# Gated unit, second half of the rows: both parts of a product (14 products of 512 columns), then four down accumulations together

## The chip, the cores and the metric

One Trainium2 chip, one of its cores. The time is device microseconds (us) of one execution of the program, from start to end. The kernel before takes 2795.59 us (median of 3 runs, 2795.36 to 2797.85).

## The reference, cut to what matters

An adaLN-conditioned block: layer norm, attention with 32 heads, residual, layer norm again, and a gated unit. The change lies in the gated unit, for 2048 rows `s`, width 576 and hidden width 4608:

```python
g = jnp.einsum("bsd,df->bsf", x, w_gate)
u = jnp.einsum("bsd,df->bsf", x, w_up)
h = _sigmoid(g) * u
return jnp.einsum("bsf,fd->bsd", h, w_down)
```

## The kernel before, in words

**Blocks and halves.** The hidden width is cut into `NB` = 18 blocks of 256, the rows into two halves of 1024. For each half and block the gate product and the up product are made as a Strassen-like scheme of seven products, in the order `ORDER = (1, 6, 2, 7, 5, 4, 3)`; the list `seq` holds all of them, and the loop `for n, (hf, b, k) in enumerate(seq)` runs one step for each.

**A product.** `product(st, k, acc, first, halves)` (L1221 to L1228) makes for each part `v` (0 is gate, 1 is up) seven matmuls of 512 columns into one PSUM bank `acc[v]`; all are line L1225. Its banks come from five that are used in turn (`product_bank`, tiles `x`). Weights of a step come by a DMA on SP's queue, asked for four steps ahead (L1197), into one of five buffers.

**The second half.** For blocks 1 to 16 (`SEVENS`) of the second half, the flag `sevens` is set and the loop goes through its own branch, 16 x 7 = 112 steps. There the down product of the block before is made by seven products too, one in each step: `sevenths(j, b, tiles)` (L1300 to L1319) makes, for each of four row tiles, one accumulation of three matmuls of 288 columns (L1307) into a bank of the pool `pd`, and adds it on VectorE to an SBUF sum (`G` at L1313, `Oa` at L1316 and L1319). `pd` has three buffers (tiles `d`), used in turn, so the accumulation of a row tile takes the bank of the one three before it, and its first weight load waits until VectorE has added that one.

```python
for t in tiles:
    acc = pd.tile([P, 512], F32, name="d")[:, 0:HALF]
    for n, (a, k) in enumerate(((h, 0), (h, 1), (l, 0))):
        nc.tensor.matmul(acc, a[:, rows], w[:, k, :], start=n == 0, stop=n == 2)
```

**What else VectorE and ScalarE do in a step of this branch.** An add of the bank of each part to an SBUF operand (L1660, in steps 6, 7, 5, 4, 3); in steps 2, 5, 4, 3 ScalarE's sigmoid of the gate part (`gate`, L1236, or L1234 for step 2) and at the step's end VectorE's product of the two parts (`gate_high`, L1242 or L1244), then ScalarE's rounded copy (L1249); `flush()` makes the rest to that copy on VectorE (`gate_low`, L1254). In step 1 `sums_of(before)` makes four sums of the block before on VectorE, in two pieces: s1 and s2 (L1335, L1336) ahead of the first product, S4 and s3 (L1340, L1341) at the second `next(made)`; S4 needs s2, s2 needs s1, s1 needs step 3's product of the two parts. `high` (L1322) copies each of them on ScalarE, `low` (L1327) makes its rest on VectorE in steps 6, 2 and 7. In step 1 ScalarE also copies the two banks to `p1` (L1668, L1676).

**The order.** From step 7 of `seq` on a manual schedule holds TensorE, VectorE and ScalarE to the order in which the program writes their instructions; nothing is moved by a planner. Each engine works its own queue in order and waits for the others by semaphores. SP's and POOL's queues carry the DMAs.

**Names used below.** p0 and p1 are the seven matmuls of part 0 and of part 1. t0 to t3 are the four row tiles of a step's down accumulations, and "the add of t0" is VectorE's add for it. add0 and add1 are VectorE's adds of the two parts at L1660.

Of the kernel before, what the change touches and what calls it, by code (L numbers as in the profile page):

```python
# [15 lines left out]
F32 = mybir.dt.float32  # L16
# [7 lines left out]
P = 128  # L24
# [37 lines left out]
TURNS = {1: 1, 6: 2, 2: 4, 7: 3, 5: 5, 4: 7, 3: 6}  # L62
# [25 lines left out]
def tile_block(ctx, tc, x_in, wqkv, wo, w_gate, w_up, w_down, c_in, w_mod, out):  # L88
    nc = tc.nc
# [911 lines left out]
    def load_block(pool, b, k, tied=None):  # L1001


        f0 = b * 256
        r0 = k * HALF
        raw = pool.tile([P, 2, 3, 256], F32, name=f"raw{k}", bufs=1 + k)
        queue = nc.gpsimd if tied else nc.sync
        for v, w in enumerate((w_gate, w_up)):
            loads = queue.dma_start(
                raw[:, v, 0:2, :], w[r0 : r0 + 256, f0 : f0 + 256].rearrange("(t p) c -> p t c", p=P)  # L1010
            ), queue.dma_start(
                raw[:, v, 2, :],
                w[r0 + 256 : r0 + HALF, f0 : f0 + 256].unsqueeze(0).to_broadcast([4, 32, 256]),
            )
            if tied:
                for load in loads:
                    tied(load)
        return raw
# [20 lines left out]
    for u in range(UNITS):  # L1039
        half, p = divmod(u, H // 2)  # L1040
# [5 lines left out]
        for kt in range(NT):  # L1046
# [43 lines left out]
            if u in (1, 3):  # L1090
                if kt == 0:
                    a = big.tile([P, 8, 640], F32, name="big")
                    a = a.rearrange("p a b -> p (a b)")[:, 0 : 8 * D].rearrange("p (t c) -> p t c", t=4)
                    b = slots.tile([P, 2560], F32, name="w0")[:, 0 : 2 * D]
# [21 lines left out]
            if u == 30 and kt == 7:  # L1116
                first = [load_block(raws, b, k, paced) for b, k in ((0, 0), (0, 1), (1, 1))]
# [31 lines left out]
    def region(name):  # L1149
        return ctx.enter_context(tc.tile_pool(name=name, bufs=1))  # L1150

    ep = region("ep")
# [68 lines left out]
    def product(st, k, acc, first, halves=(0, 1)):  # L1221
        s, w = ORDER.index(k), st["w", k]
        for v in halves:
            for n, (a, b) in enumerate(((0, 0), (0, 3), (3, 0), (1, 1), (1, 4), (4, 1), (2, 2))):
                nc.tensor.matmul(  # L1225
                    acc[v], w[:, v, a, :], X[s][:, b, :],
                    start=first and n == 0, stop=n == 6, skip_group_check=not first,
                )  # L1228

    def gate(st, t):  # L1230

        if t is None:
            t = ep2.tile([P, 512], F32, name="sg")
            nc.scalar.activation(t, st["a"][0], AF.Sigmoid)  # L1234
        else:
            nc.scalar.activation(t[:, 0:512], t[:, 0:512], AF.Sigmoid)  # L1236
        return t
# [14 lines left out]
    def gate_low(st, t, f, r):  # L1252

        nc.vector.tensor_sub(st["hl", r][:, f, :], t, st["hh", r][:, f, :].bitcast(F32))  # L1254
# [13 lines left out]
    def rows_of(j):  # L1268

        r, f = {1: (0, 0), 2: (0, 1), 4: (1, 1), 5: (1, 0)}.get(j, (None, None))  # L1270
        if r is None:
            i = {3: 0, 6: 1, 7: 2}[j]
            return late["hx"][:, i, :], late["lx"][:, i, :]
        return late["hh", r][:, f, :], late["hl", r][:, f, :]

    def columns_of(j):

        q = {1: (0, 0), 2: (1, 0), 3: (1, 1)}.get(j)
        if q:
            return late["wd"][:, :, q[0], q[1] * HALF : (q[1] + 1) * HALF]  # L1280
        i = {5: 0, 6: 1, 7: 2, 4: 3}[j]
        return late["wt"][:, i // 2, :, i % 2, :]
# [17 lines left out]
    def sevenths(j, b, tiles):  # L1300

        (h, l), w = rows_of(j), columns_of(j)
        for t in tiles:
            rows = slice(t * P, (t + 1) * P)
# [3 lines that stand above are left out]
            if j in late["G"]:  # L1308
                to = late["G"][j][:, t, :]
                if b == 0:  # L1310
                    nc.vector.tensor_copy(to, acc)
                else:
                    nc.vector.tensor_add(to, to, acc)  # L1313
            elif j == 4:
                to = Oa[:, 4 + t, 0:HALF]
                nc.vector.tensor_sub(to, to, acc)  # L1316
            else:
                to = Oa[:, t, 0:HALF] if j == 2 else Oa[:, t, HALF:D]
                nc.vector.tensor_add(to, to, acc)  # L1319
# [5 lines left out]
    def low(j):  # L1325
        h, l = rows_of(j)
        nc.vector.tensor_sub(l, late.pop(("t", j)), h.bitcast(F32))  # L1327

    def sums_of(st):

        a11, a12, a21, a22 = st["t", 0, 0], st["t", 1, 0], st["t", 0, 1], st["t", 1, 1]
        s1, s2, s3 = (
            sums[k].tile([P, 2, 3, P], F32, name=f"S{k}").rearrange("p v t c -> p (v t c)")[:, 0:512] for k in (1, 2, 3)
        )
        nc.vector.tensor_add(s1, a21, a22)  # L1335
        nc.vector.tensor_sub(s2, s1, a11)  # L1336
        high(5, s1)
        high(6, s2)
        yield
        nc.vector.tensor_sub(late["S4"], a12, s2)  # L1340
        nc.vector.tensor_sub(s3, a11, a21)  # L1341
        high(3, late["S4"])
        high(7, s3)
        yield
# [84 lines left out]
    def block(n):  # L1429
        half, b, _ = seq[n]  # L1430
        if (half, b) not in blocks:
            blocks[half, b] = {"b": b, "half": half}
            if half == 0:
                for k in range(2):
                    load(b, k)
                blocks[half, b]["raw"] = [loaded.pop((b, k)) for k in range(2)]
        return blocks[half, b]
# [165 lines left out]
    def half(t, v):  # L1603
        return t[:, 512 * v : 512 * (v + 1)]
# [5 lines left out]
    def flush():  # L1610
        while behind:
            gate_low(*behind.pop())

    for n, (hf, b, k) in enumerate(seq):
# [7 lines left out]
        st, kept = block(n), None  # L1622
# [5 lines left out]
        if sevens:  # L1628
            if at or b > 1:
                load_columns(b if at else b - 1, TURNS[seq[n - 1][2]])  # L1630
            if b == 1 and k in (1, 6, 2, 7):
                load_columns(0, {1: 3, 6: 5, 2: 7, 7: 6}[k])
            if k == 1:
                made = sums_of(before)
                next(made)
                st["a"], first = banks(), True
                acc, to, by = st["a"], None, None
            elif k == 6:
                st["b_"], first = banks(), True
                st["u2"] = ep.tile([P, 1024], F32, name="u2")  # L1640
                acc, to, by = st["b_"], st["u2"], st["p1"]
            elif k == 2:
                acc, first, to = st["a"], False, None
                for r in range(2):
                    st["hh", r], st["hl", r] = late["hh", r], late["hl", r]
            elif k == 7:
                st["u3"] = ep2.tile([P, 1024], F32, name="u3")
                acc, first, to, by = st["b_"], False, st["u3"], st["p1"]
            elif k == 5:
                st["c"], first = banks(), True  # L1650
                acc, to, by = st["c"], st["u3"], st["u3"]
            elif k == 4:
                acc, first, to, by = st["b_"], False, st["p1"], st["p1"]
            else:
                acc, first, to, by = st["c"], False, st["u2"], st["u2"]
            f, r = {2: (0, 0), 5: (1, 1), 4: (1, 0), 3: (0, 1)}.get(k, (None, None))
            for v in range(2):
                product(st, k, acc, first, (v,))
                if to is not None:
                    nc.vector.tensor_add(half(to, v), acc[v], half(by, v))  # L1660
                if v == 0 and f is not None:
                    t = gate(st, to)
                sevenths(TURNS[k], b - 1, (2 * v, 2 * v + 1))
                if v == 0:
                    if k == 1:
                        next(made)
                        st["p1"] = ep.tile([P, 1024], F32, name="p1")
                        nc.scalar.copy(half(st["p1"], 0), acc[0])  # L1668
                    elif k == 6:
                        low(3)  # L1670
                    elif k == 2:
                        low(5)
                    elif k in (7, 4, 3):
                        flush()
                elif k == 1:
                    nc.scalar.copy(half(st["p1"], 1), acc[1])  # L1676
            if f is not None:
                got = gate_high(st, t, f, r)
                if got:
                    behind.append(got)  # L1680
            if k in (2, 7):
                low({2: 6, 7: 7}[k])
            if k == 3:
                before = st
                st["wd"] = late["wd"][:, 0], late["wd"][:, 1]
            continue
# [131 lines left out]
```

## Time and profile before

| | |
|---|---|
| median of 3 runs | 2795.59 us (2795.36 to 2797.85) |
| the profiled execution's own time | 2804.88 us |
| its span | 2803.1 us |
| TensorE matmul busy | 2771.9 us (99%) |
| VectorE busy | 2306.3 us (82%) |
| ScalarE busy | 1609.3 us (57%) |
| GpSimd busy | 814.6 us (29%) |
| mean granted TensorE clock | 0.998 |

The span runs from the first to the last instruction on the core; the profiled time has 1.8 us more around it. A matmul's recorded duration includes its run through the array, so that neighbours overlap: what one matmul costs is the distance from its start to the next one's start. VectorE's neighbours overlap in the same way.

### The profile page before, as it was taken

To read this page: it belongs to the slowest core of one execution; us is meant where nothing else is said; L and a number is where in the kernel's file an instruction comes from. 1 tells how busy PE (TensorE), PEld (TensorE's weight loads), DVE (VectorE), ACT (ScalarE), POOL (GpSimd) and SP (SyncE) were. 2 spreads that over 40 slices of the span, in tenths; PEclk is the share of its full clock that TensorE was granted. 3 is DMA by queue.
4 is the path that set the end of the run, shared out by engine and by line. 5 is a ranking of instruction groups with operands and counts; after the bars stand their busy time and mean duration, and the time that the engine had idled before them with its cause. 6 is when DMAs were issued, how large, how long until landed. Compare 5 with 4: busy or idle time off the path is not lost.

```text
span 2803.1 us, 50644 instructions
## 1 busy us (share of the span) xinstructions
PE 2771.9 (99%) x18637; PEld 1847.4 (66%) x18637; DVE 2306.3 (82%) x4370; ACT 1609.3 (57%) x3051; POOL 814.6 (29%) x1077
## 2 busy tenths in 40 slices
PE   7999999999999999999999999999999999999999
PEld 5975444444444444444444888888888888888888
DVE  7278999999998888999883778888898677777777
ACT  3215999999999878999888332333333222222221
POOL 3125207888843111663103222232221100000000
PEclk9999999999999999999999999999999999999999
DMA  5344224444432120232127766667767956566653
GB/s 172 121 157 140 78 61 162 171 169 166 172 133 82 36 58 24 98 106 71 43 68 227 273 222 223 240 213 273 278 245 280 339 195 201 194 200 195 200 195 120
DMA packets 170777, 462.59 MB, mean 165 GB/s; under 512 B 21212, under 2 KB 88032, under 8 KB 160416
## 3 DMA queue, kind: packets, MB, share of 16 engines
q1 hardware_dynamic: 150064, 360.72, 38.4%
q0 software_dynamic: 20464, 98.62, 9.9%
q8 instruction: 147, 2.41, 0.4%
q14 instruction: 102, 0.84, 0.1%
HBM read 281.92 MB, written 176.82 MB: 164 GB/s over the span
## 4 chain that ended last, share of the span: by engine, by line
PE 92%; DVE 4%; DMA 2%; issue 2%; POOL 0%; ACT 0%; SPq 0%; DVEq 0%; ACTq 0%; POOLq 0%
PE x L1225 26%; PE o L656 19%; PE s L1084 12%; PE s L550 11%; PE d L1375 8%; PE d L1307 6%; PE s L336 4%; PE s L805 2%; PE s L389 1%; DMA out_dram<-Oa 1%; DVE mx L556 1%; PE s L683 1%; DMA wq_raw<-in_A_wqkv_dram 1%; DVE w L1215 0%; DVE Oa L1379 0%
## 5 line engine op out<-in xcount | busy, mean ns | idle before, releaser
L1088 ACT ACTIVATE p<-s 128x512 f32<-128x512 f32 x2048 | 1069.1, 616 | 89.2 <-PE s L1084 62.6
L556 DVE TENSOR_REDUCE mx<-s 128x1 f32<-128x512 f32 x1568 | 1000.9, 683 | 101.3 <-PE s L550 75.1
L656 PE MATMUL o<-p,vaug 128*32 128x256 f32 (+1 forms) x5848 | 595.1, 478 | 0.1
L550 PE MATMUL s<-k,q 54*128 54x512 f32 x1920 | 548.6, 434 | 2.0 <-DVE t L775 1.0
L1084 PE MATMUL s<-q,k 56*128 56x512 f32 x1920 | 527.7, 440 | 0.0
L550 PEld LDWEIGHTS s<-k,q 54*128 54x128 f32 x1920 | 273.4, 184 | 231.9 <-DVE mx L561 88.0
L1084 PEld LDWEIGHTS s<-q,k 56*128 56x128 f32 x1920 | 249.8, 184 | 232.1 <-ACT p L1088 72.9
L1225 PE MATMUL x<-k,w 128*128 128x512 f32 x1512 | 370.0, 392 | 0.0
L1225 PEld LDWEIGHTS x<-k,w 128*128 128x128 f32 x1512 | 276.8, 188 | 53.3 <-PE o L656 0.8
L1375 PE MATMUL d<-wd,hh 128*128 128x288 f32 x1248 | 249.9, 295 | 2.4 <-DVE Oa L1379 2.4
L656 PEld LDWEIGHTS o<-p,vaug 128*32 128x32 f32 x5848 | 116.2, 108 | 203.1 <-issue 187.5
L1225 PE MATMUL x<-big,w 128*128 128x512 f32 x1008 | 245.5, 392 | 0.7 <-DVE u L1724 0.7
L1225 PE MATMUL x<-w,w 128*128 128x512 f32 x1008 | 245.3, 391 | 0.0
L1225 PEld LDWEIGHTS x<-big,w 128*128 128x128 f32 x1008 | 185.1, 188 | 37.0 <-DVE u L1724 1.1
L1225 PEld LDWEIGHTS x<-w,w 128*128 128x128 f32 x1008 | 184.3, 188 | 34.5
L1375 PEld LDWEIGHTS d<-wd,hh 128*128 128x128 f32 x1248 | 202.2, 188 | 6.2 <-DVE Oa L1379 3.1
L1375 PE MATMUL d<-wd,hl 128*128 128x288 f32 x624 | 184.3, 295 | 0.0
L1379 DVE TENSOR_TENSOR Oa<-Oa,d 128x288 f32<-128x288 f32 x312 | 136.6, 453 | 55.1 <-PE d L1375 51.2
L561 DVE CUSTOM_DVE_ANT_0 over<-s,over 128x512 f32<-128x512 f32 x240 | 163.9, 683 | 1.3 <-PE s L1084 1.2
L559 ACT ACTIVATE over<-s 128x512 f32<-128x512 f32 x240 | 145.8, 608 | 11.3 <-PE s L550 9.3
L1234 ACT ACTIVATE sg<-x 128x512 f32<-128x512 f32 x36 | 21.6, 599 | 210.2 <-PE x L1225 210.2
L1206 ACT CAST w<-S 128x768 fp32r<-128x768 f32 x71 | 59.4, 836 | 137.8 <-POOL S L1179 136.0
(275 smaller groups left out, 3898.5 us busy)
## 6 DMA issues: line engine op xcount, KB each, us to landing
ws<-w SPq DMA_DIRECT2D x126, 640.0 KB
w<-ws SPq DMA_DIRECT2D x126, 640.0 KB
wd<-wds SPq DMA_DIRECT2D x19, 1152.0 KB
k<-kd SPq DMA_DIRECT2D x60, 360.0 KB
wds<-w POOLq DMA_DIRECT2D x18, 1152.0 KB, 5.2
wtd<-t POOLq DMA_DIRECT2D x32, 576.0 KB, 5.0
wt<-wtd SPq DMA_DIRECT2D x64, 288.0 KB
wd<-wds SPq DMA_DIRECT2D x52, 288.0 KB
```

The source lines that it names most:

```text
L336: nc.tensor.matmul(acc, w, hT[:, t, cols], start=n == 0, stop=n == len(ts_) - 1)
L550: nc.tensor.matmul(sp, qs[rows, qt * P : (qt + 1) * P], ks[rows, at * 512 : (at + 1) * 512], start=True, stop=True,)
L556: nc.vector.tensor_reduce(to, sp, axis=AX.X, op=ALU.max)
L559: nc.scalar.activation(over, sp, AF.Relu)
L561: nc.vector.tensor_tensor_reduce(out=over, in0=sp, in1=over, scale=1.0, scalar=LOWEST, op0=ALU.add, op1=ALU.max, accum_out=mx[:, h * n + q ...
L656: nc.tensor.matmul(acc[32 * j : 32 * j + 32, cols], vaug[:, kt, (2 * p + h) * VW : (2 * p + h) * VW + 32], probs[2 * c + h][:, cols], star ...
L1084: nc.tensor.matmul(sT, ks[rows, kcols], qs[rows, c * 512 : (c + 1) * 512], start=True, stop=True)
L1088: state["exp"] = nc.scalar.activation(pr, sT, AF.Exp, scale=SCALE)
L1225: nc.tensor.matmul(acc[v], w[:, v, a, :], X[s][:, b, :], start=first and n == 0, stop=n == 6, skip_group_check=not first,)
L1307: nc.tensor.matmul(acc, a[:, rows], w[:, k, :], start=n == 0, stop=n == 2)
L1375: nc.tensor.matmul(acc[:, :HALF], a[:, f, rows], w[:, f, cols], start=n == 0, stop=n == 5)
L1379: nc.vector.tensor_add(Oa[:, t, cols], Oa[:, t, cols], acc[:, :HALF])
```

## The change

In the branch for blocks 1 to 16 of the second half, a step no longer runs part 0, two accumulations, part 1, two accumulations. It runs part 0, part 1, then all four accumulations. On VectorE the add of t0 stands before add1, the other three after it. What stood after the first two accumulations (the second piece of the sums in step 1, `low` in steps 6 and 2, `flush` in steps 7, 4, 3) now stands before part 1, so ahead of the add of t0.

```diff
-            for v in range(2):
-                product(st, k, acc, first, (v,))
-                if to is not None:
-                    nc.vector.tensor_add(half(to, v), acc[v], half(by, v))
-                if v == 0 and f is not None:
-                    t = gate(st, to)
-                sevenths(TURNS[k], b - 1, (2 * v, 2 * v + 1))
-                if v == 0:
-                    if k == 1:
-                        next(made)
-                        st["p1"] = ep.tile([P, 1024], F32, name="p1")
-                        nc.scalar.copy(half(st["p1"], 0), acc[0])
-                    elif k == 6:
-                        low(3)
-                    elif k == 2:
-                        low(5)
-                    elif k in (7, 4, 3):
-                        flush()
-                elif k == 1:
-                    nc.scalar.copy(half(st["p1"], 1), acc[1])
+            product(st, k, acc, first, (0,))
+            if to is not None:
+                nc.vector.tensor_add(half(to, 0), acc[0], half(by, 0))
+            if f is not None:
+                t = gate(st, to)
+            if k == 1:
+                next(made)
+                st["p1"] = ep.tile([P, 1024], F32, name="p1")
+                nc.scalar.copy(half(st["p1"], 0), acc[0])
+            elif k == 6:
+                low(3)
+            elif k == 2:
+                low(5)
+            elif k in (7, 4, 3):
+                flush()
+            product(st, k, acc, first, (1,))
+            sevenths(TURNS[k], b - 1, (0,))
+            if to is not None:
+                nc.vector.tensor_add(half(to, 1), acc[1], half(by, 1))
+            elif k == 1:
+                nc.scalar.copy(half(st["p1"], 1), acc[1])
+            sevenths(TURNS[k], b - 1, (1, 2, 3))
             if f is not None:
                 got = gate_high(st, t, f, r)
                 if got:
```

## Rows read from the trace of the kernel before

**Rows 1.** Busy us of each engine in windows, here the changed stretch's main part.

```profile
2230.00:2752.00 522.00, 522.00 (x2813) 456.16 (x2811) 410.35 (x821) 120.00 (x200) 0.00 (x0) 1.00 0.60 195
```

**Rows 2.** Waits of TensorE's matmuls, 2209 to 2752: total us, times, longest.

```profile
PE d L1307 <- DVE Oa L1319: 1.4, 1, 1.4
```

**Rows 3.** Timeline, PE, second half of one step: start us, us, instruction, count.

```profile
2411.28 1.77 PE L1225 MATMUL x<-big,w 128*128 128x512 f32 x7
2412.89 0.43 PE L1307 MATMUL d<-wt,hx 128*128 128x288 f32 x2
...
2413.70 1.78 PE L1225 MATMUL x<-k,w 128*128 128x512 f32 x7
```

**Rows 4.** Timeline, PE, the end of the changed stretch and what follows.

```profile
2751.76 6.55 PE L1225 MATMUL x<-k,w 128*128 128x512 f32 x28
2758.15 0.42 PE L1375 MATMUL d<-wd,hh 128*128 128x288 f32 x2
```

**Rows 5.** Timeline, PE, outside the stretch: ten matmuls of 288, then 14 of 512.

```profile
1573.72 0.42 PE L1554 MATMUL d<-w,oh 128*128 128x288 f32 x2
...
1575.05 3.35 PE L1225 MATMUL x<-w,w 128*128 128x512 f32 x14
1578.23 0.42 PE L1375 MATMUL d<-wd,hh 128*128 128x288 f32 x2
```

**Rows 6.** Timeline, PE, outside the stretch: 48 matmuls of 288, first and next.

```profile
1933.55 0.42 PE L1375 MATMUL d<-wd,hh 128*128 128x288 f32 x2
...
1939.91 6.52 PE L1225 MATMUL x<-w,w 128*128 128x512 f32 x28
```

**Rows 7.** Timeline, DVE, step 3's end and step 1 (from 2413.70) of one block.

```profile
2413.09 0.69 DVE L1660 TENSOR_TENSOR u<-x,u 128x512 f32<-128x512 f32 x1 [0.39 <-PE x L1225]
2413.70 0.81 DVE L1313 TENSOR_TENSOR G<-G,d 128x288 f32<-128x288 f32 x2
2414.43 0.68 DVE L1244 TENSOR_TENSOR u<-u 128x512 f32<-128x512 f32 x1
2415.15 0.69 DVE L1335 TENSOR_TENSOR S<-u,u 128x512 f32<-128x512 f32 x1
2415.88 0.69 DVE L1336 TENSOR_TENSOR S<-S,sg 128x512 f32<-128x512 f32 x1
2416.48 0.81 DVE L1313 TENSOR_TENSOR G<-G,d 128x288 f32<-128x288 f32 x2
2417.21 0.68 DVE L1340 TENSOR_TENSOR S<-p,S 128x512 f32<-128x512 f32 x1
2417.82 0.68 DVE L1341 TENSOR_TENSOR S<-sg,u 128x512 f32<-128x512 f32 x1
2418.42 0.81 DVE L1313 TENSOR_TENSOR G<-G,d 128x288 f32<-128x288 f32 x2
```

**Rows 8.** Timeline, all engines, accumulations of step 2; PEld is the weight load.

```profile
2424.97 0.43 PE L1307 MATMUL d<-wt,hh 128*128 128x288 f32 x2
...
2425.24 0.29 PE L1307 MATMUL d<-wt,hl 128*128 128x288 f32 x1
2425.24 0.32 PEld L1307 LDWEIGHTS d<-wt,hh 128*128 128x128 f32 x2
...
2425.57 0.86 DVE L1316 TENSOR_TENSOR Oa<-Oa,d 128x288 f32<-128x288 f32 x2 [1.32 <-PE d L1307]
```

**Rows 9.** Timeline, DVE, block 1: last add of step 2, first of step 7.

```profile
2227.00 0.46 DVE L1316 TENSOR_TENSOR Oa<-Oa,d 128x288 f32<-128x288 f32 x1 [3.05 <-DMA Oa<-x1d]
...
2229.18 0.44 DVE L1319 TENSOR_TENSOR Oa<-Oa,d 128x288 f32<-128x288 f32 x1
```

**Rows 10.** Timeline, PE, block 1: the fourth accumulation of step 7, then step 5.

```profile
2229.68 0.53 PE L1307 MATMUL d<-wd,hx 128*128 128x288 f32 x2 [1.38 <-DVE Oa L1319]
2230.04 0.29 PE L1307 MATMUL d<-wd,lx 128*128 128x288 f32 x1
2230.18 1.78 PE L1225 MATMUL x<-k,w 128*128 128x512 f32 x7
```

## The prediction

> **What bounds the kernel now.** I read three views, in this order. The windows say which engine fills the changed stretch: from 2230 to 2752 us TensorE's matmuls are busy for 522.00 of 522.00 us, VectorE for 410.35 and ScalarE for 120.00 [rows 1]. The waits say what TensorE still waits for there: one wait in all 112 steps, 1.4 us, for a VectorE add [rows 2]. So the stretch lasts as long as TensorE needs to issue its matmuls, and regrouping them can gain only if a matmul then starts sooner after the one before it. The timeline gives these distances. Seven matmuls of 512 columns take 2412.89 - 2411.28 = 1.61 us and the six of 288 behind them 2413.70 - 2412.89 = 0.81 [rows 3]. From the start of step 5 of block 1 at 2230.18 [rows 10] to the end of the stretch at 2751.76 [rows 4] there are 108 steps (3 of block 1, 15 blocks of 7), so a step takes 521.58 / 108 = 4.830 us.
>
> **The change, part by part.** No matmul, add, copy or DMA is added or removed; all of it is order. The two adds, the sigmoid and the product of parts are the same instructions later or earlier in a step.
>
> *Longer runs on TensorE, a gain.* Within the stretch a matmul of 512 takes 1.61 / 7 = 0.230 to 0.231. The 28 right behind it take 2758.15 - 2751.76 = 6.39 [rows 4]; if the first seven cost 1.62 as elsewhere, the other 21 take 4.77, or 0.227 each. So a matmul of 512 is dearer in the first places after a run of 288 and then settles, and runs of seven hardly settle at all. For 14 in a row there are two nearby rows. One run of 14 behind ten matmuls of 288 took 1578.23 - 1575.05 = 3.18 [rows 5]. The first half of the 28 gives 1.62 + 7 x 0.227 = 3.21. I take 3.20, the middle. Twelve of 288 take 2 x 0.81 = 1.62 at most now; in a run of ten 1.33 x 1.2 = 1.59 [rows 5], in a run of 48 a quarter of 6.36, also 1.59 [rows 6]. A step would then take 3.20 + 1.59 = 4.79 against 4.83: 0.04 x 108 = **4.6 us gained** with the unrounded 0.043. The ends are 3.21 + 1.60 (2 gained in all) and 3.18 + 1.58 (7 gained).
>
> The Trainium skill bears on this, against the change: its page "TensorE: Matmul & The Clock Gate" (section "Wait — 56ns, not 53.3ns?") states that matmuls at the full clock start N / 2.4 GHz plus a fixed 2.5 ns apart, so that a neighbour's size plays no part. By that rule this term would be nothing. The rows disagree in that the same 512 columns take 0.231 in one place and 0.227 in another.
>
> *The fourth accumulation in a row, a wait.* Four accumulations now follow each other with three buffers, so t3 needs the add of t0 in the same step. When is it needed? The weight load of a matmul starts as the matmul before it starts (2425.24 for both [rows 8]). With a matmul of 288 every 0.1325 us, t3's first load is due 8 x 0.1325 = 1.06 after t0 begins. When does it come? From t0's beginning to its third matmul are 2425.24 - 2424.97 = 0.27, from there to VectorE's start 2425.57 - 2425.24 = 0.33 [rows 8]. The add takes 0.45, and from its end to TensorE are 0.05 to 0.06: it ended at 2229.18 + 0.44 = 2229.62 [rows 9] and TensorE went on at 2229.68 [rows 10]. In sum 1.10, so the load is 0.04 late even if VectorE is free. In the stalled row the third matmul follows the first by 2230.04 - 2229.68 = 0.36 instead of 0.27 [rows 10], so a late load takes about 0.10 before its matmul streams, against the 0.13 that it has in advance when on time. A load late by x thus costs x less 0.02 or 0.03. I take 0.02 for each of the 93 steps of the 108 that are not a step 1: **1.9 us** (0 to 4).
>
> *The same wait in step 1, where the add of t0 now stands behind all four sums.* Call S the start of step 1. In step 3 before it, VectorE does the add of t0 0.60 after t0 begins (0.27 + 0.33), then add1, t1, t2, t3 and the product of parts. Their distances are 0.36 after an add of an accumulation (two in 2414.43 - 2413.70 = 0.73) and 0.61 after an add of a part (2413.70 - 2413.09) [rows 7]. So the product starts 0.60 + 0.36 + 0.61 + 3 x 0.36 = 2.65 after t0 begins, and as t0 begins 1.59 before S, at S + 1.06. Now it is at 2414.43 - 2413.70 = S + 0.73 [rows 3, 7]. From there: s1 after 0.72, s2 after 0.73 (each waits for the one before [rows 7]), S4 after another 0.73 (it waits for s2 just as s2 for s1), s3 after 0.61, the add of t0 after 0.60 (2418.42 - 2417.82): S + 4.45. Add 0.45 and 0.05: TensorE may load at S + 4.95. It is due at S + 3.20 + 1.06 = S + 4.26. Late by 0.69, it costs 0.67, in 15 blocks **10.0 us**. The bounds: if S4 didn't have to wait for s2 (0.61 instead of 0.73) and the product started 0.05 sooner, 0.50, in all 7.5; if each of the four dependent steps were 0.03 slower, 0.79, in all 12.
>
> Behind the waiting load stand t3's three matmuls and all of step 6's first product, since TensorE works in order; add0 of step 6 slides along, so VectorE gets that time back: it has 522 - 410 = 112 us idle in the stretch, 1 us a step [rows 1], and step 6's own t0 add isn't late again. ScalarE's copies of the sums and of the two banks come later too, but ScalarE is busy for only 120 of 522 us [rows 1] and add0 of step 6, the first to need them, has moved back by the wait as well.
>
> *Block 1's first four steps.* There the only wait of the stretch stands. VectorE's add of t3 in step 2 waits for a DMA that lands just before 2227.00 and three more instructions separate it from step 7's add of t0 at 2229.18 [rows 9], for which TensorE's load waits 1.38 [rows 10]. The landing doesn't depend on the change: POOL's DMAs were asked for in block 0. With `flush` now ahead of t0, a fourth instruction (0.60) comes in between, and step 5 starts **0.6 us** later. What step 1 of this block loses is swallowed by that wait. Ends: -1 and +1.5.
>
> *At nothing.* The weights of a step four ahead need the buffer of the step just past, whose last product now ends 0.8 us earlier, so SP's queue isn't held longer; the down columns are asked for behind t3 in both orders, and used six steps later. The rests made by `flush` and `low` come before add1 instead of behind two adds; they are used a step or more later. If that cover went, the price would be seen as a wait of PEld at t0, which the sum doesn't hold.
>
> *Sum.* -4.6 + 10.0 + 1.9 + 0.6 = **+7.9 us**. The durations come from an execution with a span of 2803.1 and a time of 2804.88, 9.3 above the median of 2795.59; as the terms are differences within 4.8 us steps, I put them on the median: 2795.6 + 7.9 = **2803.5**. About 0.2%, or 5.6 us, is what a measurement of this kernel can tell from no change.
>
> **The rivals.**
>
> *The fixed price.* Runs of 14 cost twice a run of seven. Then t0 begins at S + 3.24, the load in step 1 is 0.65 late and costs 0.63, 9.5 in 15 blocks; with 1.9 and 0.6 that is +12.0, 2807.6. For it: the stretch has no run longer than seven, so no row inside it shows 0.227, and the late loads break the rhythm anew in each step. Against it: 0.227 in the 21 matmuls after the stretch [rows 4] and 3.18 for 14 [rows 5]. Chance 0.14. This is the case that the Trainium skill's fixed cost leads to.
>
> *No wait at t3 (not slower).* It decides at step 1: if the add of t0 starts by S + 3.76 (S + 4.26 less 0.50) the wait is gone there, and the gain alone stays: -4.6, 2791.0, between -7 and -1. The add would have to be 0.7 us sooner, one VectorE instruction fewer in the chain from step 3's product to t0. For it: VectorE idles 1 us a step, and now keeps the order s1, s2, two adds, S4, s3 without holding TensorE up. Against it: that order is kept to the letter [rows 7], each link is timed there, and none is left out by the change. Chance 0.12.
>
> *VectorE falls behind everywhere.* If `flush` or `low` ahead of t0 is late by a ScalarE copy (the rest in step 7 needs the copy made after step 2's product of parts), t0's add comes 0.15 late in all steps, not 0.04: 93 x 0.13 = 12 instead of 1.9, near +18 to +20, 2815. Against it: from that product's start, at S + 1.06 of the next step or before, to t0's add, due at S + 3.20 + 0.60 = S + 3.80, are 2.7 us for one copy by ScalarE, which is busy for only 120 of 522 us [rows 1], add0 and one rest. Chance 0.08.
>
> **How the numbers follow.** The forecast has 0.66, with its own range from +2 to +14 by the bounds above; two thirds of it lie above 5.6, so 0.45 slower and 0.21 the same. The fixed price gives 0.13 and 0.01, falling behind 0.08 slower, no wait 0.07 the same and 0.05 faster. Slower 0.66, same 0.29, faster 0.05. The range runs from +1 to +15.5, 2796.5 to 2811: it takes in the forecast's bounds and the fixed price, and leaves out falling behind and most of no wait, with the tails 0.2.
>
> **What the profile after would show.** Right: runs of 14 matmuls at L1225 in 3.18 to 3.21 us; in each step 1 from block 2 on one wait of PEld at L1307 for a VectorE add, matmuls pushed back by some 0.6 to 0.7 us, with L1341 right ahead of that add; 0.00 to 0.04 at t3 of other steps; the stretch from 2230 to its end about 7 us longer. Wrong: no wait in step 1 (the chain is shorter than I read), runs of 14 in 3.24 (no gain), waits over 0.1 in other steps (VectorE or ScalarE is late), or a wait at t0 of any step, which no term holds.

## The result and the profile after

The changed kernel takes 2810.31 us (median of 6 runs, 2807.6 to 2813.26); the kernel before, beside it, 2798.45 (6 runs, 2795.36 to 2802.03). The ratio is 1.0039, 95% interval 1.0028 to 1.0049: 0.0039 x 2798.45 = 10.9 us slower. In the experiments it ran again and gave 1.0046 (1.0033 to 1.0059).

| | before | changed |
|---|---|---|
| median | 2798.45 us | 2810.31 us |
| profiled execution: time, span | 2804.88, 2803.1 | 2807.6, 2805.8 |
| TensorE matmul busy | 2771.9 us | 2769.1 us |
| VectorE busy | 2306.3 us | 2309.7 us |
| the 112 steps, first product to the end | 542.42 us | 549.76 us |

The profiled execution before took longer than any of the six runs timed beside the changed kernel, so the spans aren't to be compared: they differ by 2.7 us, the medians by 12. Its stretch of 542.42 us is also the longer of two lengths that this kernel shows, as the last experiments tell.

The windows of the stretch after, from 2225 to 2754 us, in the columns of [rows 1]:

```profile
2225.00:2754.00 529.00, 523.09 (x2806) 457.67 (x2805) 411.71 (x818) 120.06 (x200) 0.00 (x0) 1.00 0.63 193
```

TensorE's matmuls are busy for 523 of 529 us where they filled every one of 522. Who it waits for is in the waits of its weight loads from 2200 to 2770 us (total us, times, longest); before there was one such wait in the stretch [rows 2]:

```profile
PEld d L1307 <- DVE G L1313: 9.4, 15, 0.6
PEld d L1307 <- DVE G L1311: 1.1, 1, 1.1
```

One wait in each of the 16 steps 1, none elsewhere that is long enough to be listed. The timeline of VectorE in step 1 of block 2, whose first product starts at S = 2239.32, answers to [rows 7]:

```profile
2240.38 0.68 DVE L1244 TENSOR_TENSOR u<-u 128x512 f32<-128x512 f32 x1
2241.09 0.69 DVE L1335 TENSOR_TENSOR S<-u,u 128x512 f32<-128x512 f32 x1
2241.82 0.69 DVE L1336 TENSOR_TENSOR S<-S,sg 128x512 f32<-128x512 f32 x1
2242.55 0.69 DVE L1340 TENSOR_TENSOR S<-p,S 128x512 f32<-128x512 f32 x1
2243.16 0.69 DVE L1341 TENSOR_TENSOR S<-sg,u 128x512 f32<-128x512 f32 x1
2243.76 1.66 DVE L1313 TENSOR_TENSOR G<-G,d 128x288 f32<-128x288 f32 x4
```

And TensorE's timeline of the same step:

```profile
2239.32 3.38 PE L1225 MATMUL x<-k,w 128*128 128x512 f32 x14
2242.53 0.42 PE L1307 MATMUL d<-wd,hh 128*128 128x288 f32 x2
...
2243.58 0.29 PE L1307 MATMUL d<-wd,hl 128*128 128x288 f32 x1
2244.26 0.53 PE L1307 MATMUL d<-wd,hh 128*128 128x288 f32 x2 [0.39 <-DVE G L1313]
2244.63 0.29 PE L1307 MATMUL d<-wd,hl 128*128 128x288 f32 x1
2244.76 1.09 PE L1225 MATMUL x<-k,w 128*128 128x512 f32 x4
```

The product of parts starts at S + 1.06, the four sums follow, and the add of t0 comes at 2243.76, S + 4.44. The load of t3 was due when t2's last matmul started, 2243.58, and came at 2244.26, 0.68 late:

```profile
2244.26 0.30 PEld L1307 LDWEIGHTS d<-wd,hh 128*128 128x128 f32 x2 [0.62 <-DVE G L1313]
```

The last four starts span 2244.76 - 2243.58 = 1.18 us, against 4 x 0.133 = 0.53 undisturbed: 0.65 lost, 9.8 us in 15 blocks. Busy time hides part of a wait: the listed idle time is 0.39, since the matmul before still runs through the array at first and the late matmul's record begins at 2244.26 with its weight load, not when it streams.

In the other steps t3 loses little; here a step 2, t2 and t3 of it, then t3's weight load:

```profile
2253.57 0.43 PE L1307 MATMUL d<-wt,hh 128*128 128x288 f32 x2
2253.84 0.29 PE L1307 MATMUL d<-wt,hl 128*128 128x288 f32 x1
2253.97 0.45 PE L1307 MATMUL d<-wt,hh 128*128 128x288 f32 x2
2254.26 0.29 PE L1307 MATMUL d<-wt,hl 128*128 128x288 f32 x1
```

```profile
2253.88 0.30 PEld L1307 LDWEIGHTS d<-wt,hh 128*128 128x128 f32 x2
```

The load was due at 2253.84 and is 0.04 late, as forecast. From first to third matmul t2 takes 0.27 and t3 0.29: about 0.02 lost.

### The profile page after: what moved, and what is told of

The parts are those of the page before. It is cut to its first block, busy times and chain, and to the rows that moved or that the text cites. A ratio compares the mean times of both kernels' runs of the same rounds, so it can differ in the third digit from the quotient of the medians.

```text
span 2805.8 us, 50612 instructions
## 1 busy us (share of the span) xinstructions
PE 2769.1 (99%) x18637; PEld 1847.2 (66%) x18637; DVE 2309.7 (82%) x4370; ACT 1609.2 (57%) x3051; POOL 814.7 (29%) x1077
## 4 chain that ended last, share of the span: by engine, by line
PE 90%; DVE 7%; issue 1%; DMA 1%; ACT 0%; SPq 0%; POOL 0%; DVEq 0%; ACTq 0%; POOLq 0%
PE x L1225 25%; PE o L656 19%; PE s L1084 12%; PE s L550 11%; PE d L1375 8%; PE d L1307 5%; PE s L336 4%; PE s L805 2%; PE s L389 1%; DVE G L1313 1%; DVE mx L556 1%; PE s L683 1%; DMA wq_raw<-in_A_wqkv_dram 0%; DVE u L1244 0%; DVE S L1335 0%
## 5 line engine op out<-in xcount | busy, mean ns | idle before, releaser
L1225 PE MATMUL x<-k,w 128*128 128x512 f32 x1512 | 360.0, 391 | 0.0
L1225 PE MATMUL x<-big,w 128*128 128x512 f32 x1008 | 239.4, 391 | 0.7 <-DVE u L1726 0.7
L1225 PE MATMUL x<-w,w 128*128 128x512 f32 x1008 | 239.1, 391 | 0.0
```

The lines of the kernel that those rows point to most:

```text
L1225: nc.tensor.matmul(acc[v], w[:, v, a, :], X[s][:, b, :], start=first and n == 0, stop=n == 6, skip_group_check=not first,)
```

## The experiments

Ratios are to the kernel before, timed on the same chip beside each (27 runs with the first four experiments, median 2799.55; 21 with the next four, 2797.13).

| | median us | ratio (95%) | 112 steps, us |
|---|---|---|---|
| sums behind the add of t0 | 2802.48 | 1.0013 (1.0005 to 1.0022) | 540.90 |
| changed, four and four banks | 2792.11 | 0.9976 (0.9967 to 0.9985) | 536.95 |
| before, four and four banks | 2794.13 | 0.9986 (0.9977 to 0.9995) | 538.76 |
| changed again | 2811.17 | 1.0046 (1.0033 to 1.0059) | 551.12 |
| changed, s3 twice | 2820.45 | 1.0077 (1.0059 to 1.0096) | 561.22 |
| before, four and four, padded | 2793.50 | 0.9979 (0.9970 to 0.9988) | 535.56 |
| changed, four and four, padded | 2794.40 | 0.9986 (0.9977 to 0.9995) | 537.34 |
| before, profiles 2, 3, 4 | 2798.75, 2804.47, 2796.07 (one run each) | | 538.31, 542.55, 537.47 |

**The sums behind the add of t0.**

```diff
             if k == 1:
-                next(made)
                 st["p1"] = ep.tile([P, 1024], F32, name="p1")
...
             sevenths(TURNS[k], b - 1, (0,))
+            if k == 1:
+                next(made)
```

> The changed kernel with one line moved: in step 1 the second piece of the sums (S4, s3) stands behind the add of t0 again, as before the change; the four accumulations stay together. Main theory (t3 waits for the add of t0, which the sums hold up): the 15 or 16 waits of some 0.55 us in step 1 go, 9 us in all; the small waits at the fourth accumulation stay (0.02 to 0.03 in a step, 2.5 in all) and the runs of 14 keep their gain (4 to 5), so 1 to 3 us below the kernel before, stretch of 112 steps near 540 us against 542.4 before and 549.8 changed. Rival (the fourth accumulation is late whatever stands ahead, since VectorE has fallen behind): the waits in step 1 shrink by less than half and the time stays 4 us or more above before. Rival (regrouping itself costs outside the waits): about 10 us above before less 9, so still slower by 1 to 2.

The waits in step 1 are gone; of the weight loads' waits in the stretch one is left, in block 1, and VectorE's add of t0 now waits for TensorE, not TensorE for it:

```profile
PEld d L1307 <- DVE Oa L1319: 1.2, 1, 1.2
```

```profile
2276.60 0.69 DVE L1336 TENSOR_TENSOR S<-S,sg 128x512 f32<-128x512 f32 x1
2277.88 0.46 DVE L1313 TENSOR_TENSOR G<-G,d 128x288 f32<-128x288 f32 x1 [0.59 <-PE d L1307]
2278.25 0.69 DVE L1340 TENSOR_TENSOR S<-p,S 128x512 f32<-128x512 f32 x1
```

The stretch lost 549.76 - 540.90 = 8.9 us of its 549.76, as the main theory had it. But the time is 0.0013 x 2799.55 = 3.6 us above before where 1 to 3 below were expected: the gain of the longer runs didn't show in the medians. Against two of the three later profiles of the kernel before, 537.47 and 538.31, this stretch is 2.6 to 3.4 us longer, which is near the 3.6 of the medians.

**Four banks for the accumulations and four for the products,** in the changed order and, as a control, in the old one.

```diff
-    products = [ctx.enter_context(tc.tile_pool(name=f"pg{i}", bufs=1, space=PSUM)) for i in range(5)]
-    products = sorted(range(5), key=lambda i: (i - turns["bank"] - 1) % 7), products
+    products = [ctx.enter_context(tc.tile_pool(name=f"pg{i}", bufs=1, space=PSUM)) for i in range(4)]
+    products = sorted(range(4), key=lambda i: (i - turns["bank"] - 1) % 7), products
...
-        i = products[0][turns["x"] % 5]
+        i = products[0][turns["x"] % 4]
...
-    pd = ctx.enter_context(tc.tile_pool(name="pd", bufs=3, space=PSUM))
+    pd = ctx.enter_context(tc.tile_pool(name="pd", bufs=4, space=PSUM))
```

> The changed kernel with four PSUM banks for the accumulations and four for the products instead of three and five. Main theory: each accumulation now takes the bank of the same row tile one step before, so no wait for a VectorE add is left in the stretch, neither the 0.55 us in step 1 nor the 0.025 elsewhere; what stays is the gain of longer runs: 0.04 us a step, 4 to 5 us below the kernel before, steps of 4.79 us, runs of 14 in 3.19 to 3.20 us. Rival (fixed price of a matmul, runs of 14 as dear as two of 7): the waits go, but the time is that of the kernel before, steps of 4.83. Rival (four product banks are too few): new waits of L1225 for adds of the parts, time above before.

> The kernel before with the same four and four banks, as the control of the run above. Main theory: the stretch has no wait for VectorE before (but one of 1.4 us in block 1), so nothing changes: within 1 us of the kernel before, steps of 4.83 us. If the banks were what makes the run above fast, this one would be faster as well; if four product banks are too few it is slower by the same amount as the run above falls short.

With four banks no wait is left in the changed order; its windows show TensorE filling the stretch again:

```profile
2222.00:2739.00 517.00, 517.00 (x2805) 454.56 (x2804) 411.57 (x820) 120.17 (x200) 0.00 (x0) 1.00 0.65 197
```

From step 5 of block 1 to the end it takes 517.79 us, 4.794 a step, as expected, and the time is 6.7 us below before, where 4 to 5 were expected. The control fell out otherwise than expected: it is faster as well, by 0.0014 x 2799.55 = 3.9 us. One part lies ahead of the stretch, in the steps of the first half. The waits of the accumulations' weight loads for VectorE in the kernel before, from 1530 to 2209 us, and then in the control, 1530 to 2201:

```profile
PEld d L1375 <- DVE Oa L1379: 3.1, 3, 1.8
...
PEld d L830 <- DVE Oa L1379: 1.1, 2, 0.6
...
PEld d L1554 <- DVE Oa L1379: 0.7, 2, 0.3
```

```profile
PEld d L1375 <- DVE Oa L1379: 1.0, 1, 1.0
```

Three banks made TensorE wait there too; the fourth takes back about 3.9 of those 4.9 us. In the stretch the control takes 538.76 against the 542.42 of the first profile. Block 1's first four steps, with the wait of [rows 10], are 0.5 us shorter; the other 3.1 us lie in the 108 steps behind them, where the kernel before has no wait that could have gone. So the steps of the old order aren't always 4.83, and between the two orders with four banks only 0.001, 2 to 3 us, is left, and their intervals overlap.

**The changed kernel once more.**

> The changed kernel itself once more. The stretch of 112 steps is 7.3 us longer in its profile than in the one before, the medians differ by 11 to 12 us with an interval of 7.8 to 13.7. Main theory (all of the difference lies in the stretch): 7 to 9 us above before. Rival (something outside the stretch costs 3 to 4 us as well): 11 to 12 again, and the profile shows the stretch near 549.8 us and the rest longer than in the kernel before.

The ratio is 1.0046, 12.9 us, and the stretch 551.12, 8.7 above the first profile before. The part outside, with the first 2205 us and the last 51, is no longer than in that profile. Neither theory fits, as long as 542.42 stands for the kernel before.

**One more VectorE instruction ahead of the add of t0.**

```diff
         nc.vector.tensor_sub(s3, a11, a21)
+        nc.vector.tensor_sub(s3, a11, a21)
```

> The changed kernel with s3 written twice in step 1 (the same instruction again, one more VectorE instruction of 0.61 us ahead of the add of t0; the outputs are the same). Main theory (the wait in step 1 is as long as VectorE's chain ahead of the add of t0): each of the 15 waits grows from 0.55 by 0.61 us, 9 us in all (16 steps: 9.8 at most), so the stretch goes from 548 to 549 up to 557 to 559 and the time to about 20 us above before. Rival (VectorE has slack there, the wait has another cause): the stretch stays within 2 us.

Waits of weight loads in the stretch, and VectorE in one step 1:

```profile
PEld d L1307 <- DVE G L1313: 20.5, 15, 1.4
```

```profile
2245.94 0.68 DVE L1341 TENSOR_TENSOR S<-sg,u 128x512 f32<-128x512 f32 x1
2246.65 0.69 DVE L1342 TENSOR_TENSOR S<-sg,u 128x512 f32<-128x512 f32 x1
2247.26 1.66 DVE L1313 TENSOR_TENSOR G<-G,d 128x288 f32<-128x288 f32 x4
```

The waits grew from 9.4 to 20.5 us in 15, 0.74 each, and the stretch from 549.76 to 561.22. Of these 0.74 the rows show 0.71, where 0.61 was expected: the second writing of the same tile comes 0.71 after the first (2246.65 - 2245.94), while s3, which doesn't use S4, comes 0.61 after it (2243.16 - 2242.55 above). VectorE's chain sets the wait, link by link.

**The kernel before, profiled three more times.** Nothing was edited.

> The kernel before, looked at once more. 27 runs of it lie in groups near 2797 and 2800.5 us, and its first profile (2804.9) has a stretch of 540.8 us from its first accumulation, in which runs of seven matmuls of 512 take 1.62 and runs of six of 288 0.79 to 0.80. In the run with four banks, in the same order, most runs of seven take 1.60 and most of six 0.787. Theory A (the distances of matmuls settle into one of two rhythms, and what happens in block 1 picks it): this look shows, as most executions would, the shorter rhythm, a stretch near 537.5 us, and the change then costs 10 to 11 us in it, as the medians say. Theory B (one rhythm for each kernel): 540.8 again, and the 3 to 4 us that the medians have above the profiles lie outside the stretch.

> The kernel before, a third look. Two looks gave two rhythms (stretch 540.8 with runs of seven at 1.62, and 536.7 with 1.607). Theory A (block 1 picks one of two rhythms): either of the two again, nothing between, and in the shorter one steps 1, 6, 5, 4 take 1.600 and 0.787. Theory B (the first look was a one-off, its late weights or its clock made it longer): 536 to 537 with whatever wait in block 1.

> The kernel before, a fourth look, as the third: 536 to 538 or 540 to 541 us, and the wait in block 1 differs between the looks.

TensorE's timeline at the start of step 5 of block 1 and at the end of the stretch, in the second, the third and the fourth profile:

```profile
2227.32 0.62 PE L1225 MATMUL x<-k,w 128*128 128x512 f32 x2
...
2745.60 6.53 PE L1225 MATMUL x<-k,w 128*128 128x512 f32 x28
```

```profile
2229.74 0.63 PE L1225 MATMUL x<-k,w 128*128 128x512 f32 x2
...
2751.32 6.55 PE L1225 MATMUL x<-k,w 128*128 128x512 f32 x28
```

```profile
2224.66 0.63 PE L1225 MATMUL x<-k,w 128*128 128x512 f32 x2
...
2742.94 6.53 PE L1225 MATMUL x<-k,w 128*128 128x512 f32 x28
```

The 108 steps take 518.28, 521.58 and 518.28 us; in the first profile it was 521.58. Two values, 3.3 us apart, to the hundredth: the kernel before has two rhythms, 4.830 and 4.799 us a step. (The expectations count its stretch from the first accumulation, 1.59 us less than the table does.) The control's 538.76 is the shorter one, so nearly all of its gain stands in the waits ahead of the stretch. In the shorter one a part of a step 4 takes 1.60 and 0.79, here in the second profile:

```profile
2268.08 1.76 PE L1225 MATMUL x<-big,w 128*128 128x512 f32 x7
2269.68 0.42 PE L1307 MATMUL d<-wt,hx 128*128 128x288 f32 x2
...
2270.47 1.76 PE L1225 MATMUL x<-big,w 128*128 128x512 f32 x7
```

In block 1 the weight loads' waits differ from profile to profile: 1.6 us in the first, 0.8 in the second, two of 1.2 and 0.5 in the third, none in the fourth. The two with the longest waits have the longer rhythm, but the control has the shorter one with waits of 1.1 and 0.3. That such a wait picks the rhythm is not shown.

Which rhythm the timed runs had can be estimated from their times and mean granted clocks. Of the 27 runs the nine with 0.998 took 2798.9 to 2800.9 us, but for one of 2804.3; the first profile, 0.998 and the longer rhythm, took 2804.88, the second, 0.998 and the shorter, 2798.75. The nine with 0.999 took 2796.4 to 2797.5, but for one of 2800.7; the fourth profile, 0.999 and shorter, took 2796.07. So most of them probably had the shorter rhythm, and the groups near 2797 and 2800.5 that the expectation names go with the granted clock.

**Padding the transposed down columns,** on top of the four and four banks, in the old order and in the changed one.

```diff
-        late["wt"] = pool.tile([P, 2, 2, 2, HALF], F32R, name="wt")
+        late["wt"] = pool.tile([P, 2, 2, 2, HALF + 32], F32R, name="wt")
...
-        return late["wt"][:, i // 2, :, i % 2, :]
+        return late["wt"][:, i // 2, :, i % 2, 0:HALF]
...
```

> The kernel before with four and four banks, and the transposed down columns wt padded by 32 values, so that the second of each pair starts 1280 bytes behind the first instead of 1152: the moving columns of steps 2 and 3 then start where those of steps 1, 6, 5 and 4 start, modulo 256 bytes; those of step 7 stay 128 bytes off. Theory (a run of 288 is dearer, 0.80 against 0.787, and makes the next 512s dearer, 1.612 to 1.621 against 1.600, where its moving columns start 128 bytes off): steps 2 and 3 take 1.600 and 0.787 like the others, step 7 stays as it is; 0.12 us a block, 1.9 us less than the run with four banks alone. Rival (it goes by the step or the weights, not by the start of the columns): steps 2, 3 and 7 as before, same time.

> The changed kernel (four accumulations together) with four and four banks and the same padding. Theory (what the longer runs gain depends on the rhythm and not on the length: behind a run of twelve at 1.579 the 14 take 3.22, behind one at 1.604 they take 3.18): steps 2 and 3 go to 1.579 and the runs of 14 after them to 3.22, nothing gained, within 1 us of the changed kernel with four banks; then 7, 6, 7, 6 with padding (4.774 us a step) is cheaper than 14 and 12 (4.80). Rival (longer runs are cheaper by themselves): this one is the fastest of all, 2 us or more below the changed kernel with four banks.

First part of a step 2, from its seven to the second part's seven: without padding (the second profile of the kernel before), then padded, old order.

```profile
2284.85 1.76 PE L1225 MATMUL x<-w,w 128*128 128x512 f32 x7
2286.45 0.43 PE L1307 MATMUL d<-wt,hh 128*128 128x288 f32 x2
...
2287.25 0.63 PE L1225 MATMUL x<-w,w 128*128 128x512 f32 x2
```

```profile
2248.30 1.76 PE L1225 MATMUL x<-w,w 128*128 128x512 f32 x7
2249.90 0.42 PE L1307 MATMUL d<-wt,hh 128*128 128x288 f32 x2
...
2250.69 1.76 PE L1225 MATMUL x<-w,w 128*128 128x512 f32 x7
```

The six of 288 take 0.80 and 0.79. To the nanosecond they take 802 and 787, and the seven behind them 1.621 and 1.600 us. Steps 2 and 3 went to the cheap values, step 7, whose columns were left as they were, stayed at 0.80; here its first part, then the second part's seven, which take 1.62:

```profile
2253.08 1.76 PE L1225 MATMUL x<-w,w 128*128 128x512 f32 x7
2254.68 0.43 PE L1307 MATMUL d<-wd,hx 128*128 128x288 f32 x2
...
2255.48 1.78 PE L1225 MATMUL x<-w,w 128*128 128x512 f32 x7
```

The stretch came down by 3.2 us to 535.56, where 1.9 was expected; the rest is that no wait stood in block 1 this time. Of the three steps with dear columns the two that were moved became cheap and the one that wasn't stayed: the start of the moving columns decides, then, and not the step or its weights.

In the changed order with padding, two steps in a row:

```profile
2235.71 3.38 PE L1225 MATMUL x<-k,w 128*128 128x512 f32 x14
2238.93 0.42 PE L1307 MATMUL d<-wd,hh 128*128 128x288 f32 x2
...
2240.51 3.38 PE L1225 MATMUL x<-k,w 128*128 128x512 f32 x14
```

And without padding, behind the twelve of a step 3 (2234.44 to 2236.05, 1.61):

```profile
2236.05 3.35 PE L1225 MATMUL x<-k,w 128*128 128x512 f32 x14
2239.23 0.42 PE L1307 MATMUL d<-wd,hh 128*128 128x288 f32 x2
...
2240.81 3.38 PE L1225 MATMUL x<-k,w 128*128 128x512 f32 x14
```

Behind accumulations that padding made cheap (1.58, as 2238.93 to 2240.51) the 14 take 3.22 (2235.71 to 2238.93), behind dear ones 3.18 (2236.05 to 2239.23). What padding saves in the twelve is lost in the 14, and the stretch, 537.34, is no shorter than without (536.95); the ratio is 0.001 higher, with overlapping intervals. Longer runs aren't cheaper by themselves: 3.22 + 1.58 = 4.80 a step against 2 x (1.600 + 0.787) = 4.774 in the old order.

Four versions beat both kernels: the changed order with four and four banks (0.9976), the old order with them and padding (0.9979), the changed one with both (0.9986) and the old order with the banks alone (0.9986); their intervals overlap.

## Why the prediction was right or wrong

*Right: the direction, the range and the wait.* Slower had 0.66, the range from 2796.5 to 2811 holds 2810.31, if barely; the second timing, 2811.17, lies just above it. The size fell short: +7.9 forecast, +10.9 and +12.9 by the ratios. The chain in step 1 came out link by link: product at S + 1.06 (forecast 1.06), add of t0 at S + 4.44 (4.45), load due at 2243.58, S + 4.26 (4.26), at TensorE at S + 4.94 (4.95). The cost, 0.65 a block and 9.8 in 15, was forecast as 0.67 and 10.0. Both directions were tried: taking the two sums out of the chain ended the wait, one more link lengthened it by that link's 0.74.

*Right: the small wait elsewhere.* Forecast 0.02 a step, 1.9 in all; the run with the sums put back and the one with four banks, otherwise alike, take 520.41 and 517.79 in the 108 steps, 2.6 apart. Of that 0.5 belongs to step 1, whose last four starts span 0.560 and 0.527 us in the two runs; 2.1 is left for the other 93 steps.

*Wrong: "4.6 us gained" by longer runs, in its reason too.* Against the first profile it holds about: 4.830 us a step then and 4.794 without waits, 0.036 x 108 = 3.9. But the step of the prediction that failed stands in its sum: "as the terms are differences within 4.8 us steps, I put them on the median". A difference within a step carries over only if the other executions have that step. Two of four profiles have 4.799, and against that the gain is 0.005 x 108 = 0.5 us. Nor is it the length that pays: two cheap runs of seven take 3.200, a run of 14 takes 3.18 to 3.22. With 0.5 the sum for the 108 steps is -0.5 + 9.8 + 2.1 = +11.4; with 3.9 it is +8.0. The 108 steps themselves went from 521.58 or 518.28 to 529.48, by 7.9 or 11.2:

```profile
2224.94 0.62 PE L1225 MATMUL x<-k,w 128*128 128x512 f32 x2
...
2754.42 0.39 PE L1225 MATMUL x<-k,w 128*128 128x512 f32 x1
```

In the second profile of the changed kernel they take 530.39, 8.8 or 12.1 more. The forecast for these steps, -4.6 + 10.0 + 1.9 = +7.3, holds only against the longer rhythm, in which its rows happened to be taken. The timed ratios show 10.9 and 12.9, nearer to the difference from the shorter one.

*Wrong in kind: the 0.6 us in block 1.* The wait there comes and goes with the landing of a DMA: VectorE's adds in step 2 wait for it 3.05 us in the first profile before, 1.88 in the second, 3.08 and 1.06 in the third, 1.36 in the fourth, and not at all in the first profile after. The four steps take 20.84, 20.03, 20.97 and 19.19 us in the profiles before, 20.28 and 20.73 in the two after. No effect of the change can be told from that.

*The rivals.* No wait at t3 was wrong in every block. VectorE falling behind everywhere was wrong too: outside step 1 the add of t0 starts 0.33 after t0's third matmul, as it did before [rows 8]. The fixed price, +12.0 and 2807.6, had the wrong reason, since the same seven matmuls take 1.600 to 1.623, but its result, no gain, is nearer than mine. The Trainium skill's rule behind it ("TensorE: Matmul & The Clock Gate", section "Wait — 56ns, not 53.3ns?") has a fixed 2.5 ns on top of N / 2.4 GHz; here a settled matmul of 512 has 227 - 213 = 14 ns [rows 4], and more behind runs of 288.

## What to carry to other kernels

When accumulations are bunched, count the buffers they rotate through: with one fewer than the bunch, the last waits for the add of the first, and every instruction that the consumer's engine has ahead of that add, in program order, becomes part of the producer's path. Moving an instruction "earlier" on an in-order engine delays all that stands behind it. And before a few nanoseconds of one profiled execution are multiplied by a hundred steps, look at a second execution: the unit may have two values.

## What the runs showed of the hardware

In the old order's shorter rhythm a run of six 288-column matmuls took 786 to 787 ns or 799 to 802 (790 to 791 or 799 to 802 in the longer one), by where in memory its moving columns start: 128 bytes (1280 - 1152) moved steps 2 and 3 from the dear value to the cheap one. A run of seven of 512 behind it took 1.600 to 1.623 us, not by its own shape but by what ran before, and the state outlives a step: without padding the old order repeats its steps in one of two patterns, 33.59 or 33.81 us a block, the same in all 15 blocks behind block 1. What in the engine keeps that memory, no run here shows.
